# Two layers of grouped-query decode attention and a gated MLP: each 1 MB load of K and V issued as two transfers, of the even and of the odd partitions

## The chip, the cores and the metric

The kernel runs on one core of one Trainium2 chip. The metric is the device time of one execution in microseconds (us), the median of three runs. The profile is one further execution, recorded by the hardware profiler. Its times count from the first instruction of the program.

## What is computed

Four sequences each decode one token. A layer is attention over a cache of 4,096 positions (32 query heads, 8 heads of K and V, 128 wide) and a gated MLP, each behind a layer norm and with a residual. The two layers use the same weights and the same caches.

```python
def _A_ref(x, k_cache, v_cache, wq, wo):     # x (4, 1, 512); caches (4, 8, 4096, 128), bfloat16
    q = (x @ wq).reshape(B, Sq, Hq, Dh).transpose(0, 2, 1, 3)
    k = jnp.repeat(k_cache, rep, axis=1)
    v = jnp.repeat(v_cache, rep, axis=1)
    scores = jnp.einsum("bhqd,bhkd->bhqk", q, k) * (Dh ** -0.5)
    p = _softmax(scores, axis=-1)
    o = jnp.einsum("bhqk,bhkd->bhqd", p, v)
    return o.transpose(0, 2, 1, 3).reshape(B, Sq, Hq * Dh) @ wo

def _B_ref(x, w_gate, w_up, w_down):          # F = 1792
    h = _sigmoid(x @ w_gate) * (x @ w_up)
    return h @ w_down

x = x + _A_ref(_layernorm(x), k_cache, v_cache, wq, wo)
x = x + _B_ref(_layernorm(x), w_gate, w_up, w_down)
x = x + _A_ref(_layernorm(x), k_cache, v_cache, wq, wo)
x = x + _B_ref(_layernorm(x), w_gate, w_up, w_down)
```

K of one sequence and one head is 4,096 x 128 bfloat16 values, 1 MB, and so is V. There are 32 such pairs, and both layers read all of them.

## The kernel before, in words

A unit of work is one layer, one sequence and one head of K and V; the kernel has 64 units and takes them in pairs (32 pairs, written out in `ORDER`). The instructions of all engines are recorded by a small scheduler (`_Sched`), which turns reads and writes of named buffers into semaphore waits. The order of the steps within and between pairs is a string written by hand (`PROGRAM`), in which each letter is one step of one pair; the order of the loads is another string (`LOADS`: k, v, and o, g, u, d for weights).

One load fills one slot. A slot is 128 partitions of 4,096 values, that is 8 KB in each partition; position 32p + j of the cache lies in partition p, and so each partition's 8 KB is contiguous in HBM. There are 12 slots, and 4 more in the buffer of `wq` once layer two's queries are made (`yield_wq`, L978). Some K and V of layer one stay in their slots for layer two (`KEPT`); all others are read from HBM twice. That leaves 97 loads of 1 MB, each one transfer, and the very last V, which is read in two transfers of 512 KB, each of half the columns of all 128 partitions.

`pump` (L343) is called after every step. It takes loads from the list as long as a slot is free in the plan, and records each as one `dma_start` on SP's queue (L369) with the semaphore of its slot. All weight loads (L349 and, for `wq`, L382) are on the same queue. SP does nothing else. A load into a used slot waits on SP (its waits are recorded at L106) for the last reader of that slot: PE's score matmuls for K, PE's value matmuls for V. The queue is in order, and so a load that waits holds up all loads behind it.

The steps of one unit that touch a load:

- `k_turn` (L984, VectorE, L993) transposes the K slot in place in blocks of 32 x 32, in one to four parts. Its first part waits for the load of the slot.
- `scores` (L995, TensorE, L1009) multiplies the queries with K into PSUM; then the K slot is free.
- The maximum (L1026), its spreading (L1035), the bias (L1049, L1056), the exponential (ScalarE, L1063), the transpose of the probabilities (TensorE L1081, copies by ScalarE L1133) and the sums follow.
- `pv` (L1164, TensorE, L1179) multiplies the probabilities with V. Its first matmul waits for the V load; after its last one the V slot is free.

Between them lie the output projection (L1236, L1329), the MLP of layer one and the queries of layer two (L814, L839, L885, L934), which are done one sequence at a time beside the attention. After the last unit, the MLP of layer two ends the kernel.

The semaphore of a slot is raised by 16 by each transfer, one for each of the 16 DMA engines; `dma` (L82) records that, and `assign_values` (L85) counts what each waiter has to wait for.

Of the kernel before, what the change touches and what calls it, by code (L numbers as in the profile page):

```python
# [111 lines left out]


NSLOT = 12

# [28 lines left out]
def bass_interleave_layers__gqa_block_cached__glu_gated_glu__decode_kernel(  # L146
# [17 lines left out]
    P = 128  # L164
# [19 lines left out]
    S = _Sched()  # L184
# [4 lines left out]
    def sbt(shape, dtype, name):  # L189
        cnt[0] += 1  # L190
        return es.enter_context(nc.sbuf_tensor(f"{name}_{cnt[0]}", list(shape), dtype))
# [3 lines left out]

    slot = [sbt([P, NJ * DH], dt.bfloat16, f"slot{i}") for i in range(NSLOT)]
    wq_sb = sbt([P, KD, HQ * DH], dt.bfloat16, "wq")
# [20 lines left out]
    def small(*shape, dtype=dt.float32):  # L218
# [63 lines left out]
        list(ENGINES)  # L282
        + [f"d{i}" for i in range(NSLOT + KD)]
        + [f"wq{i}" for i in range(KD)]
# [51 lines left out]

    free = list(range(NSLOT))
    where = {}

    def take():  # L340
        return free.pop(0)

    def pump():  # L343
        while loads:
            kind, n = loads[-1]
            if kind in wparts:
                loads.pop()
                dst, src = wparts[kind](n)
                S.dma("sp", (lambda dst, src: lambda e: e.dma_start(dst, src))(dst, src), f"wo{n}" if kind == "wo" else kind, writes=[f"{kind}{n}"])  # L349
                continue  # L350
            if not free:
                return
            loads.pop()
            s = take()
            _, b, u = seq[n]
            if kind == "k":
                where["kn", n] = s
                src = A_k_cache[b, u].rearrange("(p j) d -> p (j d)", p=P)
            else:
                where["v", b, u] = s  # L360
                src = A_v_cache[b, u].rearrange("(p j) d -> p (j d)", p=P)
            parts = [(slot[s][:, :], src, f"d{s}", f"s{s}")]
            if kind == "v" and n == NU - 1:
                h = NJ * DH // 2
                parts = [(slot[s][:, 0:h], src[:, 0:h], "vh", "vh"), (slot[s][:, h:], src[:, h:], f"d{s}", f"s{s}")]
            for dst, frm, sem, key in parts:
                deps = S.readers.get(f"s{s}", []) + [S.last_write.get(f"s{s}")] if key == "vh" else ()
                S.dma(
                    "sp", (lambda dst, frm: lambda e: e.dma_start(dst, frm))(dst, frm), sem, writes=[key], deps=deps  # L369
                )  # L370

    def dve(fn, reads=(), writes=()):
        return S.inst("dve", fn, reads=reads, writes=writes)
# [5 lines left out]
    for n in range(KD // 2):  # L379
# [4 lines left out]
            writes=[f"wq{2 * n}", f"wq{2 * n + 1}"],  # L384
        )
    pump()

    S.inst("pool", lambda e: e.memset(qz_sb[:, :, :, :, :], 0.0), writes=QZ + ["pf"])
# [6 lines left out]
        writes=["pe0"],  # L395
    )
    dve(lambda e: e.transpose(pidx[:, :], iota_f[:, 0:32]), writes=["pe0"])
    for a in range(4):
# [6 lines left out]
            writes=[f"ident{a}"],  # L405
# [5 lines left out]
    for k in range(KD):  # L411
# [13 lines left out]
        writes=[f"x{b}" for b in range(Bn)],  # L425
# [552 lines left out]
    def yield_wq():  # L978
        for k in range(KD):
            S.last_write[f"s{NSLOT + k}"] = S.last_write[f"wq{k}"]  # L980
            S.readers[f"s{NSLOT + k}"] = list(S.readers[f"wq{k}"])
            free.append(NSLOT + k)

# [454 lines left out]
    head_masks()  # L1438
    k_turn(0)
    pump()  # L1440
    k_turn(1)
    pump()
    q_mm(Bn, 0, HQ)
    q_spread(0, Bn)
# [100 lines left out]
    for c in PROGRAM:  # L1545
# [29 lines left out]
        writes=["sel_row"],  # L1575
# [4 lines left out]
        writes=["rowk"],  # L1580
# [3 lines left out]
    for part in range(2):  # L1584
# [21 lines left out]
        writes=["o_row"],  # L1606
# [56 lines left out]
```

## Time and profile before

| | |
|---|---|
| three runs | 306.2, 306.71, 309.35 us; median 306.71 us |
| the profiled execution | 307.37 us, its span from the first to the last instruction 305.6 us |
| mean granted TensorE clock | 0.699 |
| busy: PE, DVE, ACT, POOL | 222.4, 193.8, 118.1, 40.3 us |
| read from HBM | 116.66 MB, 382 GB/s over the span |
| issues of 1 MB: V into slots, K into slots | 48, 44 |
| issues of 1 MB into the freed `wq` buffer: V, K | 3, 2 |
| issues of 512 KB of V | 2 |

How to read the profile. PE is TensorE's matmuls, DVE is VectorE, ACT is ScalarE, POOL is GpSimd, SP is the engine that issues the loads; a q behind a name (SPq) means the engine's sequencer, which waits and issues. L369 is line 369 of the kernel. The page cuts the span into 40 equal slices of 7.64 us; a digit is the busy share of a slice in tenths. A queue's line has packets, MB and the time that the packets took, as a share of the span of 16 engines. The chain of waits follows the work that ended last back to its start and gives each step's share of the span. A row of a table of stretches has the stretch, its length, then for PE, weight loads, DVE, ACT and POOL the busy us with the number of instructions, then the granted clock, the DMA engines' busy share and GB/s. A share of the DMA engines over 1 comes from packets whose recorded times overlap a little. A row of waits has the engine that waited and its line, what ended the wait, the us in total, how often, and the longest. The row of a line has the number of instructions and the shortest, median and longest duration in ns.

### The profile page before, as it was taken

To read this page: it belongs to the slowest core of one execution; us is meant where nothing else is said; L and a number is where in the kernel's file an instruction comes from. 1 tells how busy PE (TensorE), PEld (TensorE's weight loads), DVE (VectorE), ACT (ScalarE), POOL (GpSimd) and SP (SyncE) were. 2 spreads that over 40 slices of the span, in tenths; PEclk is the share of its full clock that TensorE was granted. 3 is DMA by queue.
4 is the path that set the end of the run, shared out by engine and by line. 5 is a ranking of instruction groups with operands and counts; after the bars stand their busy time and mean duration, and the time that the engine had idled before them with its cause. 6 is when DMAs were issued, how large, how long until landed. Compare 5 with 4: busy or idle time off the path is not lost.

```text
span 305.6 us, 11315 instructions
## 1 busy us (share of the span) xinstructions
PE 222.4 (73%) x4872; PEld 150.2 (49%) x4872; DVE 193.8 (63%) x414; ACT 118.1 (39%) x413; POOL 40.3 (13%) x205
## 2 busy tenths in 40 slices
PE   1223565147769699999899689885789799887886
PEld 1221243124636366647456556543556574564575
DVE  6344966254513587598946486757696777678443
ACT  1001152223503257731546625334466423557600
POOL 0002111001100212111113010112021010321000
PEclk9999999999995555557756556595555576657555
DMA  7999999999999999999999999999999999999930
GB/s 292 417 426 406 409 408 381 388 419 410 415 406 409 365 388 375 425 420 417 417 417 415 416 324 416 419 402 415 420 421 418 389 368 371 365 421 423 415 132 3
DMA packets 20361, 117.38 MB, mean 384 GB/s; under 512 B 1876, under 2 KB 5976, under 8 KB 7640
## 3 DMA queue, kind: packets, MB, share of 16 engines
q1 hardware_dynamic: 20288, 116.66, 95.0%
q8 instruction: 38, 0.62, 0.8%
q14 instruction: 11, 0.09, 0.1%
q10 hardware_dynamic: 24, 0.01, 0.0%
HBM read 116.66 MB, written 0.00 MB: 382 GB/s over the span
## 4 chain that ended last, share of the span: by engine, by line
DMA 50%; PE 29%; DVE 10%; issue 4%; SPq 3%; ACT 2%; POOL 1%; DVEq 0%; POOLq 0%; ACTq 0%
DMA slot<-in_A_v_cache_dram 18%; DMA slot<-in_A_k_cache_dram 15%; DMA wq<-in_A_v_cache_dram 11%; PE S_ps L1009 8%; DVE slot L993 8%; PE O_ps L1179 7%; DMA wd<-in_B_w_down_dram 6%; PE M_ps L885 3%; SPq L369 2%; PE M_ps L839 2%; PE M_ps L934 2%; DVE small L1026 1%; PE M_ps L814 1%; ACT pT L1133 1%; PE PT L1081 1%
## 5 line engine op out<-in xcount | busy, mean ns | idle before, releaser
L993 DVE STREAM_TRANSPOSE slot<-slot 128x1024 f32<-128x1024 f32 (+2 forms) x70 | 105.0, 1507 | 18.6 <-DMA slot<-in_A_k_cache_dram 15.3
L1133 ACT ACTIVATE pT<-PT 32x128 bf16<-32x128 f32 x236 | 63.1, 268 | 57.8 <-PE PT L1081 27.8
L1009 PE MATMUL S_ps<-slot,qz 128*16 128x256 bf16 x992 | 62.1, 398 | 18.3 <-DVE slot L993 8.1
L1179 PE MATMUL O_ps<-pT,slot 128*128 128x4 bf16 x1792 | 57.0, 166 | 21.2 <-DMA slot<-in_A_v_cache_dram 13.5
L1179 PEld LDWEIGHTS O_ps<-pT,slot 128*128 128x128 bf16 x1792 | 52.9, 103 | 34.9 <-DMA slot<-in_A_v_cache_dram 17.7
L1063 ACT ACTIVATE wide<-S_ps,small 128x256 bf16<-128x256 f32 x64 | 30.3, 473 | 44.6 <-DVE small L1056 18.9
L1009 PEld LDWEIGHTS S_ps<-slot,qz 128*16 128x16 bf16 x992 | 27.8, 113 | 39.1 <-DVE slot L993 10.7
L709 POOL COPY qz<-qs 32x32 bf16<-32x32 bf16 x128 | 26.0, 203 | 110.6 <-ACT qs L694 52.8
L1026 DVE TENSOR_REDUCE small<-S_ps 128x2 bf16<-128x512 f32 x32 | 21.7, 678 | 17.3 <-PE S_ps L1009 15.4
L1081 PE MATMUL PT<-ident_bf,wide 128*128 128x64 bf16 (+1 forms) x288 | 18.7, 227 | 3.4 <-ACT wide L1063 3.3
L1081 PEld LDWEIGHTS PT<-ident_bf,wide 128*128 128x128 bf16 x288 | 15.2, 122 | 10.0 <-ACT wide L1063 8.1
L1210 DVE TENSOR_TENSOR oT<-O_ps,small 128x8 bf16<-128x8 f32 (+1 forms) x32 | 5.3, 166 | 22.3 <-PE O_ps L1179 21.5
L1092 POOL CAST small<-small 128x2 bf16<-128x2 f32 x32 | 5.9, 184 | 99.0 <-ACT wide L1063 82.1
L1049 DVE SCALAR_TENSOR_TENSOR O_ps<-O_ps,small,wide 128x128 f32<-128x128 f32 x32 | 11.2, 349 | 8.7 <-PE O_ps L1035 6.8
L885 PE MATMUL M_ps<-wq,small 128*1 128x512 bf16 x128 | 14.6, 598 | 0.0
L1236 PE MATMUL AC<-wo,oT 128*1 128x512 bf16 x96 | 11.4, 576 | 2.1 <-DMA wo<-in_A_wo_dram 1.9
L1063 ACT ACTIVATION_READ_ACCUMULATOR wide<-S_ps,small 128x1 f32 x64 | 12.3, 193 | 0.0
L694 ACT ACTIVATE qs<-M_ps 128x128 bf16<-128x128 f32 x8 | 1.9, 280 | 25.0 <-PE M_ps L683 24.9
L1035 PE MATMUL O_ps<-ident_bf,small 128*128 128x64 bf16 x64 | 8.6, 225 | 4.1 <-DVE small L1026 1.8
L1056 DVE TENSOR_REDUCE small<-O_ps 128x2 f32<-128x128 f32 x32 | 9.3, 292 | 3.2 <-ACT wide L1063 0.5
L900 ACT ACTIVATE t_row<-M_ps,small 128x512 bf16<-128x512 f32 x4 | 2.7, 687 | 21.4 <-PE M_ps L885 18.7
L1147 PEld LDWEIGHTS O_ps<-small 128*128 128x128 bf16 x124 | 6.1, 107 | 7.7 <-POOL qz L709 1.7
(142 smaller groups left out, 209.4 us busy)
## 6 DMA issues: line engine op xcount, KB each, us to landing
slot<-in_A_v_cache_dram SPq DMA_DIRECT2D x48, 1024.0 KB, 9.8
slot<-in_A_k_cache_dram SPq DMA_DIRECT2D x44, 1024.0 KB, 11.4
wq<-in_A_wq_dram SPq DMA_DIRECT2D x2, 2048.0 KB, 10.0
wo<-in_A_wo_dram SPq DMA_DIRECT2D x8, 512.0 KB, 17.6
wq<-in_A_v_cache_dram SPq DMA_DIRECT2D x3, 1024.0 KB, 10.2
wq<-in_A_k_cache_dram SPq DMA_DIRECT2D x2, 1024.0 KB, 13.0
wu<-in_B_w_up_dram SPq DMA_DIRECT2D x2, 896.0 KB, 10.6
wg<-in_B_w_gate_dram SPq DMA_DIRECT2D x2, 896.0 KB, 10.6
```

The costliest lines, as they stand in the source:

```text
L709: (lambda a, ps: lambda e: e.tensor_copy(qz_sb[ps, :, :, a, :], qs_sb[b][ps, :, u * REP:(u + 2) * REP].rearrange("p t (u r) -> p u t r", r ...
L885: (lambda k, st: lambda e: e.matmul(M_ps[h][32 * st:32 * st + 1, :], lhsT=xc_bf[:, k, 0:1], rhs=wv[:, k, h, :, st, :], start=(k == 0), sto ...
L993: dve(lambda e: e.transpose(kf, kf), writes=[f"s{st}"])
L1009: (lambda t, b2, e_, c, x1, r0: lambda e: e.matmul(S_ps[p][r0:r0 + 4 * REP, half], lhsT=qz_sb[:, part, t, :, :].rearrange("p a r -> p (a r)"),
L1026: dve(lambda e: e.tensor_reduce(rm_bf, S_ps[p].rearrange("p (u n) -> p u n", u=2), AX.X, ALU.max), reads=[f"S{p}"], writes=["rmb"])
L1049: lambda e: e.scalar_tensor_tensor(out=shifted, in0=maxima, scalar=rowk_f, in1=mask_f.rearrange("p n w -> p (n w)").unsqueeze(1).broadcast ...
L1056: dve(lambda e: e.tensor_reduce(nm_sb, shifted, AX.X, ALU.min), reads=[f"O{n}"], writes=["nm"])
L1063: (lambda u, half: lambda e: e.activation(pe_sb[:, half], S_ps[p][:, half], ACTF.Exp, bias=nm_sb[:, u:u + 1], scale=exp_scale, accum_out=s ...
L1081: (lambda w, a0, a1, c0: lambda e: e.matmul(PT[:, c0:c0 + 16 * (a1 - a0)], lhsT=wide_sb[:, NV + 64 * w:NV + 64 * w + P], rhs=valid_bf[:, : ...
L1133: (lambda dst, frm: lambda e: e.activation(dst, frm, ACTF.Copy))(dst, frm),
L1179: (lambda n, x, c, j: lambda e: e.matmul(bank[:, ul * REP:(ul + 1) * REP], lhsT=vv[:, x * JG + c * 4 + j, :], rhs=pT[:, x % 2, ul, j, 2 * ...
L1236: (lambda r, h, i: lambda e: e.matmul(AC[32 * r:32 * r + 1, :], lhsT=oT_sb[:, h, own_column:own_column + 1], rhs=wo_sb[:, h, :], start=(j ...
```

## The change

Every 1 MB load of K and V becomes two `dma_start`s of 64 partitions each, first the even ones (0, 2, 4, ...), then the odd ones. Both are on SP's queue, one right behind the other, and both raise the semaphore of the slot by 16. The first carries the waits for the slot; whoever reads the slot waits for the count of the second. The last V keeps its two transfers of 512 KB. The weights' loads, the order of loads, slots and all other engines' instructions are the same.

```diff
+PIECES = 2
...
             for dst, frm, sem, key in parts:
                 deps = S.readers.get(f"s{s}", []) + [S.last_write.get(f"s{s}")] if key == "vh" else ()
-                S.dma(
-                    "sp", (lambda dst, frm: lambda e: e.dma_start(dst, frm))(dst, frm), sem, writes=[key], deps=deps
-                )
+                n = 1 if kind == "v" and len(parts) > 1 else PIECES
+                for h in range(n):
+                    rows = slice(h, P, n)
+                    issue = (lambda dst, frm: lambda e: e.dma_start(dst, frm))(dst[rows, :], frm[rows, :])
+                    if h == 0:
+                        S.dma("sp", issue, sem, writes=[key], deps=deps)
+                    else:
+                        S.last_write[key] = S.dma("sp", issue, sem)
```

## The prediction

> **What bounds the kernel now.** I read the page's busy line of the DMA engines first, then the queue totals, the chain, the stretches of time, and last what the issuing queue SP waits for.
>
> ```profile
> DMA  7999999999999999999999999999999999999930
> GB/s 292 417 426 406 409 408 381 388 419 410 415 406 409 365 388 375 425 420 417 417 417 415 416 324 416 419 402 415 420 421 418 389 368 371 365 421 423 415 132 3
> DMA packets 20361, 117.38 MB, mean 384 GB/s; under 512 B 1876, under 2 KB 5976, under 8 KB 7640
> ...
> q1 hardware_dynamic: 20288, 116.66, 95.0%
> ```
>
> The 16 DMA engines are busy in every slice but the last two, and SP's queue alone fills 95.0% of their span. Engines that never idle cannot be helped by more requests; only fewer or cheaper packets help. The chain says the same: half of it is transfers.
>
> ```profile
> DMA 50%; PE 29%; DVE 10%; issue 4%; SPq 3%; ACT 2%; POOL 1%; DVEq 0%; POOLq 0%; ACTq 0%
> DMA slot<-in_A_v_cache_dram 18%; DMA slot<-in_A_k_cache_dram 15%; DMA wq<-in_A_v_cache_dram 11%; PE S_ps L1009 8%; DVE slot L993 8%; PE O_ps L1179 7%; DMA wd<-in_B_w_down_dram 6%; PE M_ps L885 3%; SPq L369 2%; PE M_ps L839 2%; PE M_ps L934 2%; DVE small L1026 1%; PE M_ps L814 1%; ACT pT L1133 1%; PE PT L1081 1%
> ```
>
> The stretches show where the stream is full and where it runs short (last two columns: DMA share and GB/s).
>
> ```profile
> 92.00:120.00 28.00, 25.02 (x503) 15.20 (x502) 17.41 (x36) 12.26 (x43) 5.43 (x27) 0.50 0.99 381
> 120.00:172.00 52.00, 45.88 (x990) 30.63 (x991) 36.19 (x81) 25.98 (x90) 8.80 (x44) 0.60 1.01 418
> 172.00:186.00 14.00, 11.64 (x277) 8.82 (x274) 11.68 (x26) 6.10 (x21) 1.43 (x7) 0.61 0.96 362
> 186.00:240.00 54.00, 42.94 (x971) 28.82 (x972) 38.08 (x69) 25.47 (x91) 8.95 (x45) 0.57 1.01 417
> 240.00:266.00 26.00, 23.66 (x444) 14.64 (x445) 20.10 (x46) 10.04 (x34) 3.66 (x18) 0.63 0.96 365
> 266.00:292.00 26.00, 21.98 (x557) 16.05 (x549) 17.66 (x36) 16.10 (x59) 4.32 (x22) 0.57 1.01 418
> ```
>
> Full means 417 to 418 GB/s. Three stretches run short (381, 362, 365 GB/s): there the queue is nearly empty because SP waits for a slot that PE has not released. Against 417 they lose 28 x (1 - 381/417) = 2.4, 14 x (1 - 362/417) = 1.8 and 26 x (1 - 365/417) = 3.2 us, 7.5 us in all (rounded terms differ by 0.1). That is all that a change to the transfers could win there.
>
> ```profile
> SPq L106 <- PE O_ps L1179: 93.1, 36, 11.0
> SPq L106 <- PE S_ps L1009: 47.1, 16, 5.6
> ```
>
> SP spends 93.1 + 47.1 us of the span waiting for PE: it has time to spare for more issues.
>
> **The change, part by part.** 97 loads of 1 MB (48 + 44 into slots, 3 + 2 into the freed weight buffer) become 194 pieces of 64 partitions. The last V load, already two pieces of 512 KB, and all weight loads stay. The instruction order of SP's queue keeps each pair together, so nothing is moved past another transfer.
>
> *Packets.* In the trace's packet records an 8,192 B packet takes 309 ns (median of 12,433) and the 4 B packet that counts the semaphore 9 ns (median of 1,861). A load is 128 rows, 8 per engine: 8 x 309 + 9 = 2,481 ns. Its two pieces are 2 x (4 x 309 + 9) = 2,490 ns. So +9 ns a load on each engine, 97 x 9 = 0.87 us if every load lies in a full stretch. 24 loads are issued in the three short stretches, where the engines have gaps; without them it is 73 x 9 = 0.66 us. I take 0.9, since the loads around the stretches are full.
>
> *Is there a gap between two pieces?* The trace has one row near it: the last V load's two pieces of 512 KB. Their first engines' semaphore counts come at 289.51, 290.77 and 292.04 us (the load ahead, piece one, piece two): 1.26 and 1.27 us apart, against 8 packets of 4,096 B at 159 ns + 9 = 1.28 us. So consecutive transfers follow each other without a gap: zero. The upper bound is the start of an empty queue, issue at 0.72 us to first weight packet at 1.74 us, 1.0 us, 97 times = 99 us; the lower bound is 0. I take 0, since the pieces are queued like the row that shows none.
>
> [...]
>
> *SP's issues.* The issue of a load takes 0.33 us (median), and the next begins 0.05 us later.
>
> ```profile
> L369 SPq DMA_DIRECT2D slot<-in_A_v_cache_dram x48: 327/328/5861, 1.6 to 266.8; - x48
> L369 SPq DMA_DIRECT2D slot<-in_A_k_cache_dram x44: 327/328/10571, 2.2 to 261.5; - x44
> ...
> DMA to landing us min/median/max: 5.4/10.6/27.7
> ```
>
> 97 x 0.38 = 37 us more on SP, inside the 140 us that it waits. Two issues, 0.76 us, still hand over 1 MB faster than the engines move it (2.48 us), and a load lands a median 10.6 us after its issue, behind others. Where the queue is short, the second piece reaches the engines 0.38 us after the first, which has 4 x 309 = 1.24 us of data: the engines don't run out. Cost 0; bounds 0 and 24 x 0.38 = 9.1 us, if every load of the short stretches landed late by an issue. [...]
>
> *Waits.* DVE's transpose (L993) and PE's value product (L1179) now wait for the second piece's count, 32 a load instead of 16. Both pieces are needed, so the wait ends when the last of the 1 MB has landed, as before. Behind L993 stand DVE's reductions and PE's scores; they are late only by what the landing is late.
>
> *Instruction fetch.* The page's 38 fetches of 16 KB bring 0.62 MB for 11,315 instructions, 55 B each; 97 more are 5.3 KB, a third of a fetch, at about 1.0 us on one engine. Bounds 0 and 1.0 us; I take 0, as one engine's delay fades in the next short stretch.
>
> *Sum.* 0.9 + 0 + 0 + 0 = +0.9 us. The profiled execution took 307.37 us (span 305.6, 1.8 around it), so it would become 308.3; the median of the runs, 306.71, is 0.7 lower than that execution: 307.6 us.
>
> **The rivals.**
>
> *An exposed second issue (slower).* In the three short stretches each load reaches PE or DVE late, the slot is released late, and the next load is issued late. Price up to 9.1 us: 306.7 + 0.9 + 9.1 = 316.7. For it: there SP's issues follow PE's releases, and PE is busy 89% in the first and 91% in the last. Against it: 0.38 is less than 1.24. It decides if the second piece starts later than the first one's data ends, above 1.24 us. Chance 0.12.
>
> *Pieces that don't stream at full rate (slower).* No transfer of 64 partitions stands in this trace, so how its rows are dealt to engines is not shown. If two engines met at one place of the memory throughout, each row would take twice as long: 97 x 2.48 = 241 us more, 548 us; a gap of 1.0 us gives 406 us; a rate lost by a tenth 24 us, 332 us. Against it: the 512 KB pieces and every other shape here stream back to back. It decides if 8,192 B packets rise above 309 ns by more than 4 ns (1.3%, 3 us). Chance 0.07.
>
> [...]
>
> *A quicker restart (faster).* After an idle moment, first packets take up to 1.6 us instead of 0.309 (around 179.6 us). If half-size transfers get started sooner and win half of the 7.5 us, it is 306.7 + 0.9 - 3.7 = 303.9. Against it: the consumer still waits for both pieces, and the wait for the memory is not shortened. Chance 0.08.
>
> That the split is not carried out is excluded: SP's list of the changed kernel has the pairs, 64 x 4096 each.
>
> **How the numbers follow.** The forecast case has 0.70, at 306 to 309.5; 0.03 is left for scatter beyond that. About 1% (3.1 us) is what a measurement of this kernel can tell from no change: its three runs lie between 306.2 and 309.35. Slower by over 1%, above 309.8: the second rival whole, 0.07, most of the first, 0.10, and 0.02 of scatter, 0.19. Faster, below 303.6: most of the third, 0.06 (with 0.01 of scatter). Within 1%: the rest, 0.75. The range, 304 to 313, takes in the forecast, most of the quicker restart and the lower half of the exposed issue, and leaves out about 0.15.
>
> **What would show it.** Right: 8,192 B packets still 309 ns; about 1,550 more 4 B packets (97 x 16); full stretches at 415 to 418 GB/s; SP's waits for PE shorter by about 37 us; landings of paired pieces 1.24 us apart. Wrong: rates below 410 GB/s in the full stretches (second rival); short stretches that grow while the full ones stay (first rival); short stretches that vanish (third).

## The result, and the profile after

The changed kernel takes 308.38 us (median of 20 runs, 306.24 to 310.57); the kernel before, run beside it, takes 306.69 us (20 runs). The ratio is 1.0069, with a 95% interval from 1.0046 to 1.0092: 0.0069 x 306.69 = 2.1 us more, between 1.4 and 2.8 us. The ratio leaves out executions that lie more than 1.5% above the fastest of their kernel; the medians lie 1.7 us apart, and the means of all 20 runs of each kernel (308.55 and 307.09 us) 1.5 us. That is less than the 1% that the prediction calls no change, but the interval is clear of 1. The predicted 307.6 us is 0.8 us below the measured median.

The profiled execution of the changed kernel took 310.57 us, the slowest of its 20, with a span of 308.7 us; that of before took 307.37 us. Their difference of 3.2 us is therefore larger than that of the medians, and where a stretch differs by a microsecond between the two, part of it is scatter.

The page of the changed kernel, the lines of the DMA engines and of SP's queue:

```profile
DMA  7999999999999999999999999999999999999920
GB/s 294 418 425 410 408 405 379 390 419 401 406 412 378 360 382 364 418 423 382 419 408 361 425 340 418 420 356 415 418 419 420 418 392 383 379 428 420 411 82 3
DMA packets 21914, 117.40 MB, mean 380 GB/s; under 512 B 3428, under 2 KB 7528, under 8 KB 9192
...
q1 hardware_dynamic: 21840, 116.67, 94.5%
```

Packets under 512 B grew from 1,876 to 3,428. That is 1,552 = 97 x 16, one more 4 B packet for each load on each engine, and nothing else changed in size. In the packet records the 8,192 B packets still take 309 ns (median of 12,434) and the 4 B ones 9 ns (median of 3,413). At before's median for each size, a mean engine of before has 278.6 us of SP's packets, and one of after 279.5 us.

The same six stretches of the changed kernel (length, then PE, weight loads, DVE, ACT and POOL, the clock, the DMA share and GB/s):

```profile
92.00:120.00 28.00, 25.21 (x503) 15.45 (x503) 17.42 (x37) 12.08 (x43) 5.43 (x27) 0.50 0.98 372
120.00:172.00 52.00, 42.99 (x934) 28.48 (x934) 35.96 (x81) 25.20 (x89) 8.79 (x44) 0.63 1.00 401
172.00:186.00 14.00, 11.97 (x274) 8.86 (x275) 10.08 (x24) 7.04 (x24) 1.43 (x7) 0.53 0.98 374
186.00:240.00 54.00, 43.26 (x989) 28.99 (x986) 39.32 (x69) 24.36 (x88) 8.57 (x43) 0.59 1.00 410
240.00:266.00 26.00, 22.41 (x444) 14.66 (x445) 18.57 (x44) 9.30 (x31) 3.23 (x16) 0.63 0.98 389
266.00:292.00 26.00, 21.04 (x495) 14.47 (x487) 17.79 (x32) 16.35 (x60) 4.76 (x24) 0.57 1.01 421
```

The rate is lower in three stretches (372, 401, 410 GB/s) and higher in the other three: the moments with a nearly empty queue lie elsewhere. Two cuts through the middle of the full stretches show such moments, at a DMA share of 1.00 and 0.98 where before had 1.01 and 1.00 (418 and 406 GB/s):

```profile
132.00:146.00 14.00, 11.95 (x253) 7.62 (x251) 11.89 (x25) 3.96 (x13) 1.09 (x6) 0.62 1.00 400
200.00:212.00 12.00, 9.49 (x217) 5.37 (x210) 8.01 (x13) 5.12 (x18) 2.00 (x10) 0.78 0.98 372
```

SP's view, first the issues (shortest, median, longest in ns), then its waits for PE:

```profile
L372 SPq DMA_DIRECT2D slot<-in_A_v_cache_dram x96: 471/596/5508, 1.7 to 273.8; - x96
L372 SPq DMA_DIRECT2D slot<-in_A_k_cache_dram x88: 471/597/5032, 3.0 to 268.3; - x88
...
DMA to landing us min/median/max: 3.9/9.2/21.5
```

```profile
SPq L106 <- PE O_ps L1185: 59.3, 25, 9.7
SPq L106 <- PE S_ps L1015: 37.0, 15, 4.6
```

An issue of 64 partitions takes 0.47 us behind a wait and 0.60 us behind another issue, where one of 128 took 0.33 us behind a wait and 0.43 us and up right behind another (16 of K and V, median 0.55 us). A load thus holds SP for 0.47 + 0.05 + 0.60 = 1.12 us, not the 0.33 + 0.05 + 0.33 = 0.71 us that the prediction's figures give. SP's waits for PE at L106 shrank from 140.2 to 96.3 us. SP still has time over.

### The profile page after: what moved, and what is told of

It reads as the page before. It is cut to its first block, busy times and chain, and to the rows that moved or that the text cites. A ratio compares the mean times of both kernels' runs of the same rounds, so it can differ in the third digit from the quotient of the medians.

```text
span 308.7 us, 11412 instructions
## 1 busy us (share of the span) xinstructions
PE 220.8 (72%) x4872; PEld 149.6 (48%) x4872; DVE 193.6 (63%) x414; ACT 118.1 (38%) x413; POOL 40.3 (13%) x205
## 4 chain that ended last, share of the span: by engine, by line
DMA 45%; PE 24%; DVE 14%; SPq 8%; issue 4%; ACT 2%; POOL 1%; DVEq 0%; POOLq 0%; ACTq 0%
DMA slot<-in_A_k_cache_dram 19%; DMA slot<-in_A_v_cache_dram 18%; DVE slot L999 10%; PE O_ps L1185 7%; PE S_ps L1015 7%; SPq L372 6%; DMA wd<-in_B_w_down_dram 5%; DMA wq<-in_A_v_cache_dram 3%; PE M_ps L891 2%; SPq L350 2%; ACT pT L1139 2%; DVE small L1032 1%; PE O_ps L1335 1%; POOL qz L715 1%; PE AC L1268 1%
## 5 line engine op out<-in xcount | busy, mean ns | idle before, releaser
L999 DVE STREAM_TRANSPOSE slot<-slot 128x1024 f32<-128x1024 f32 (+2 forms) x70 | 105.0, 1507 | 19.7 <-DMA slot<-in_A_k_cache_dram 16.4
L1015 PE MATMUL S_ps<-slot,qz 128*16 128x256 bf16 x992 | 60.2, 391 | 17.4 <-DVE slot L999 9.2
L1015 PEld LDWEIGHTS S_ps<-slot,qz 128*16 128x16 bf16 x992 | 26.7, 111 | 37.8 <-DVE slot L999 12.4
L1087 PEld LDWEIGHTS PT<-ident_bf,wide 128*128 128x128 bf16 x288 | 15.3, 122 | 10.1 <-ACT wide L1069 8.2
## 6 DMA issues: line engine op xcount, KB each, us to landing
wo<-in_A_wo_dram SPq DMA_DIRECT2D x8, 512.0 KB, 16.4
wq<-in_A_v_cache_dram SPq DMA_DIRECT2D x8, 512.0 KB, 14.1
```

The costliest lines, as they stand in the source:

```text
L999: dve(lambda e: e.transpose(kf, kf), writes=[f"s{st}"])
L1015: (lambda t, b2, e_, c, x1, r0: lambda e: e.matmul(S_ps[p][r0:r0 + 4 * REP, half], lhsT=qz_sb[:, part, t, :, :].rearrange("p a r -> p (a r)"),
L1087: (lambda w, a0, a1, c0: lambda e: e.matmul(PT[:, c0:c0 + 16 * (a1 - a0)], lhsT=wide_sb[:, NV + 64 * w:NV + 64 * w + P], rhs=valid_bf[:, : ...
```

## The theories

*Packets alone* (the prediction): the 4 B packets cost 97 x 9 ns, 0.9 us, and everything else is hidden. *SP's time*: the longer issues make loads late where the queue is short, and that is the rest of the 2.1 us. *Half rate*: pieces of 64 partitions move at half the rate of whole loads, the prediction's second rival.

## The experiments

Each ratio is to the kernel before, run on the same chip beside it, with its 95% interval.

### SP's time alone, half a microsecond a load

```diff
                 S.dma("sp", ..., sem, writes=[key], deps=deps)
+                if len(parts) == 1:
+                    S.group("sp", [lambda e: [e.wait_ge(sems["xin"], 16) for _ in range(17)] and None])
```

> The kernel before with whole loads, and after each of the 97 loads SP executes 17 waits that are already satisfied, about 47 ns each in the trace of after (17 ns and a gap of 30), so 0.8 us more on SP a load, about what the split adds there (0.47 + 0.60 + 0.05 us in place of 0.33). No packet is added. If SP's longer issues are what made the change cost more than its packets: 1.001 to 1.006 of the time before. If only the packets cost: 1.000, within 0.002.

Measured: 308.32 us, ratio 1.0038 (1.0003 to 1.0073). Two waits went into one instruction, and so the loss was 0.5 us a load and not 0.8: an estimate from nine instructions at 0.06 us, the time that each of thirteen takes in SP's records of the kernel with 26 waits ahead of all 97 loads, below (0.77 us from 136.30 to 137.07 us). The value is in the range of SP's time, but the interval almost reaches 1. These waits stand behind a load and ahead of SP's wait for the next slot, so they use SP's time without making a load late that SP has to wait for: SP's waits for PE at L106 are 83.9 us here, 140.2 before.

### Four pieces

`PIECES = 4`, so `rows = slice(h, P, 4)`: 32 partitions a piece.

> Four pieces of 32 partitions a load (every fourth partition). If only the 4-byte packets cost, 27 ns a load more than before, 97 times: 2.6 us, ratio 1.0085. If SP's issues count: four issues of about 0.6 us are 2.5 us a load, as long as its 2.48 us of transfer, so SP can no longer refill the queue after a wait for a slot and becomes the bound: at least 10 us more than before, ratio over 1.03, with the engines no longer full between 120 and 172 us.

Measured: four runs of 318.9 to 326.3 us, median 324.55, with 307.07 before; they scatter too far for an interval. At least 11.8 us more, against 2.6 us of packets. The page of this kernel has 1,876 + 97 x 3 x 16 = 6,532 packets under 512 B, 8,192 B packets still at 309 ns, and SP at its limit:

```profile
L372 SPq DMA_DIRECT2D slot<-in_A_v_cache_dram x192: 468/594/5012, 1.7 to 295.8; - x192
L372 SPq DMA_DIRECT2D slot<-in_A_k_cache_dram x176: 468/594/2971, 4.2 to 284.7; - x176
```

```profile
120.00:172.00 52.00, 44.41 (x928) 28.66 (x920) 36.69 (x80) 23.93 (x84) 8.87 (x44) 0.57 0.99 384
```

```profile
SPq L1617 <- DVE slot L1608: 14.4, 1, 14.4
SPq L106 <- PE O_ps L1185: 9.7, 7, 5.8
```

Its waits for PE are down from 140 us to about ten, issues back to back fill its queue, and the stretch that was full at 418 GB/s has 384. So SP has almost no time left at four issues a load; how much of the loss that explains is taken up below, with the kernels of more waits.

### Two pieces by columns

```diff
-                    rows = slice(h, P, n)
-                    issue = (lambda dst, frm: lambda e: e.dma_start(dst, frm))(dst[rows, :], frm[rows, :])
+                    w = NJ * DH // 2
+                    cut = slice(h * w, (h + 1) * w) if n > 1 else slice(0, w)
+                    issue = (lambda dst, frm: lambda e: e.dma_start(dst, frm))(dst[:, cut], frm[:, cut])
```

> Two pieces a load by columns: all 128 partitions, 4,096 B of each. The packets then take 2 x (8 x 159 + 9) = 2,562 ns a load in place of 2,481, so 97 x 81 ns = 7.9 us more by the packets alone: ratio 1.022 to 1.026. If two issues a load cost something beside it, over 1.026. The issues of 128 contiguous partitions should be as short as before (0.33 us, 0.43 us back to back) if the partition step makes the pieces' issues long.

Measured: 315.77 us, ratio 1.0254 (1.0189 to 1.0319), 7.8 us (5.8 to 9.8; the medians lie 8.7 us apart), where the packets alone give 7.9. The way of counting packets holds within those 2 us; the closer agreement is luck. The issues took 0.33 us, and 0.43 us back to back: 128 partitions were issued faster than 64 (0.47 and 0.60 us), with rows of 4,096 B as with rows of 8,192 B.

### Two pieces of adjacent partitions

`rows = slice(h * P // n, (h + 1) * P // n)`: partitions 0 to 63, then 64 to 127.

> Two pieces a load of partitions 0 to 63 and 64 to 127. If the place of the rows doesn't matter: as the change, 307 to 310 us. [...] The issues show whether a contiguous set of 64 partitions is issued in 0.33 us or in 0.47 and 0.60 us as the even and odd ones.

Measured: 497.75 us, one run, with 307.07 before: 191 us more. The page:

```profile
GB/s 340 232 232 239 230 223 218 223 227 225 375 239 217 223 228 231 227 229 228 231 243 241 233 251 250 253 248 243 246 263 274 280 261 229 221 221 227 231 225 13
DMA packets 21914, 117.40 MB, mean 237 GB/s; under 512 B 3428, under 2 KB 7528, under 8 KB 9192
...
q1 hardware_dynamic: 21840, 116.67, 97.6%
```

The packets are the same in number and size as in the changed kernel; 8,192 B packets now take 574 ns (median) and not 309, and the rate falls to 217 to 280 GB/s while K and V are read. 97 x 8 x (574 - 309) ns = 206 us, about what was lost. So which 64 partitions a piece has sets its rate here: 574 ns a packet for adjacent ones, near the rival of half rate, and 309 ns for even and odd ones. What slows the adjacent ones is not shown.

### The split where the queue is short, and where it is full

```diff
+SHORT = {*range(23, 35), *range(54, 59), *range(80, 87)}
-                n = 1 if kind == "v" and len(parts) > 1 else PIECES
+                n = PIECES if len(parts) == 1 and (nth[0] in SHORT) else 1
+                nth[0] += 1
```

and `not in SHORT` for the second kernel.

> The change for 24 loads only: those that the profile of before issues in the three short stretches (92 to 120, 172 to 186, 240 to 258 us). If the second piece and the longer issues make loads late where the queue is nearly empty: +1.0 to +2.5 us, ratio 1.003 to 1.008. If only the packets cost: 24 x 9 ns = 0.2 us, ratio 1.000 to 1.002.

> The change for the other 73 loads, which are issued while earlier transfers still fill the queue. Packets: 73 x 9 ns = 0.7 us, ratio 1.002. If late issues cost only where the queue is nearly empty, no more than that: 1.000 to 1.004. If SP's lost time counts in the full stretches too (the queue has less in it when SP next has to wait): 1.004 to 1.008.

Measured: short stretches alone 307.8 us, ratio 1.0034 (0.9998 to 1.0069); all others alone 307.74 us, ratio 1.0007 (0.9977 to 1.0037). Neither is clear of 1. Added they give 0.41%, with an interval of about 0.47% to each side (the two half-widths combined as a root of squares), which holds both 0.28% of packets and the measured 0.69%. The order of the two is that of SP's time theory, but their intervals overlap, and by the medians (306.67 us before) they cost the same, 1.1 us each.

### Whole loads with 0.8 us of waits on SP ahead of each, in the short stretches, in the others, in all

```diff
+                late = 26 if len(parts) == 1 and nth[0] in SHORT else 0
-                    "sp", (lambda dst, frm: lambda e: e.dma_start(dst, frm))(dst, frm), sem, writes=[key], deps=deps
+                    "sp",
+                    (lambda dst, frm, late: lambda e: (
+                        [e.wait_ge(sems["xin"], 16) for _ in range(late)], e.dma_start(dst, frm)
+                    )[1])(dst, frm, late),
+                    sem, writes=[key], deps=deps,
```

with `not in SHORT` for the second and no condition for the third.

> Whole loads; the same 24 loads are each issued about 0.8 us late, by 26 satisfied waits on SP after the wait for the slot (two are packed into an instruction, 0.06 us each). No packet is added. If a late issue is exposed in the short stretches: between 2 us (every tenth of it) and 19 us (all of it), ratio 1.007 to 1.06. If the queue hides it there: within 0.3% of before.

> Whole loads; the other 73 loads are each issued about 0.8 us late, 58 us of SP's time. If a late issue costs only where the queue is nearly empty: within 0.3% of before. If lost time on SP counts wherever SP waits for slots: 1.005 or more.

> Whole loads, each of the 97 issued about 0.8 us late by 26 satisfied waits on SP: the time that the change adds on SP, before the load itself, and no packet. If SP's time is what the change costs beyond its packets (0.69% measured, 0.28% packets): ratio 1.002 to 1.006. If the packets and something else in the transfers cost all of it: 1.000 to 1.002.

Measured: 1.0026 (0.9992 to 1.0059), 1.0018 (0.9987 to 1.0049) and, for all, 1.0016 (0.9983 to 1.0049). For all 97 loads the upper end is 0.49%.

These runs did not do what was expected of them. In the program that ran, SP's wait for the slot stands behind the satisfied waits, just ahead of the load. One load of the kernel with all 97 shows it in SP's records: from 136.30 us on come thirteen satisfied waits of 17 to 28 ns, at 137.07 us one that takes 2,231 ns because it also holds PE's semaphore, and at 139.34 us, 0.04 us after its end, the issue. The profile counts that wait among the added ones: the longest on their line takes 10 us, and SP's waits for PE stand there too, 100.8 us of them in place of 140.2.

```profile
L372 SPq EVENT_SEMAPHORE  x1326: 17/28/10049, 2.4 to 269.8; - x190
```

```profile
SPq L372 <- PE O_ps L1184: 61.3, 29, 10.1
SPq L372 <- PE S_ps L1014: 39.5, 16, 5.4
```

So a load that SP has to wait for was not made late by the added waits; they took their time out of SP's wait. Of the 24 loads of the short stretches SP waited for the slot of all 24 before, and still for 17 here; all 17 were issued within 0.11 us of the wait's end. The other 7 found their slot free, and how late they were the records don't tell. The time in which such waits held SP ahead of the 24 (those over 0.11 us in its records) went from 67.5 to 47.6 us, by about the 19 us that the waits add. With waits ahead of all 97 loads it went from 169 to 108 us. What the three kernels show is that SP can lose 0.8 us a load ahead of its waits for less than 0.6% of the time. What it costs when a load that SP waits for goes out late, once its slot is free, they don't show. Only the kernels with pieces have that, and there 24 split loads in the short stretches cost at most 0.69%.

### More waits

The last kernel with 46 and with 69 waits.

> The same with 46 waits, about 1.4 us a load: SP then needs 1.8 us a load against 2.48 us of transfer. If the cost grows in proportion to SP's lost time: 0.7 to 1.0%. If it grows faster once SP has little time over: 1 to 3%.

> The same with 69 waits, about 2.1 us a load: SP then needs 2.5 us a load, as with four pieces, and as long as the transfer. If the 17 us of the four pieces come from SP's time, all but their 2.6 us of packets: 12 to 17 us more than before, ratio 1.04 to 1.055. If they come from the smaller pieces in the transfer engines: under 1.02.

Measured: 46 waits cost 1.0131 (1.0097 to 1.0164), 69 waits 1.0207 (1.0145 to 1.0269), 6.4 us. Here too the wait for the slot comes last. The cost is below 0.5% at 0.8 us a load and 1.0 to 1.6% at 1.4 us. Waits for slots hold SP for 67 and 21 us, ahead of 36 and 17 of the 97 loads (71 before); the others find their slot free when SP reaches them.

The kernel with 2.1 us needs as much SP time a load as that with four pieces, but loses 6.4 us (4.5 to 8.3), where the four pieces lose at least 11.8 - 2.6 = 9.2 us beside their packets. So some 3 us (1 to 5) of the four pieces' loss, or more, is not SP's lost time as these waits make it. Two differences could account for that, and neither was tried by itself. The pieces stand behind the wait for the slot, and the added waits ahead of it. And each piece hands over 2 x 309 + 9 = 627 ns of work, less than the 640 ns from one issue to the next (a median 594 ns and the 0.05 us behind it), so engines could run dry between pieces, an estimate from these figures.

### The change with 0.8 us of waits ahead of each load

The changed kernel with 26 waits ahead of each first piece. The wait for the slot again stands behind them.

> The change, and each load's first piece issued about 0.8 us late by 26 satisfied waits. If the longer issues of the pieces use up the same spare time of SP as the waits do, SP loses 0.8 + 0.8 = 1.6 us a load: between the 1.3% of 1.4 us and the 2.1% of 2.1 us, about 1.5%, and 0.3% of packets, 1.6 to 2.0% over before. If the change's cost beyond its packets lies in the transfers and not on SP: its 0.7% and the 0.2% that 0.8 us cost with whole loads, 0.7 to 1.1%.

Measured: 307.4 us, ratio 1.0017 (0.9977 to 1.0057). Both forecasts miss: SP's time theory wanted 1.6 to 2.0%, the other 0.7 to 1.1%, and the upper end is 0.57%. Its page shows that the waits and pieces are there, and SP's longest waits:

```profile
SPq L378 <- PE O_ps L1192: 27.5, 12, 7.9
SPq L1624 <- DVE slot L1615: 22.5, 1, 22.5
SPq L378 <- PE S_ps L1022: 11.5, 11, 2.9
```

SP waits for PE about 40 us and not 140, having lost 1.6 us a load, and the kernel is no slower than the split alone. So SP's total time is not, by itself, what costs: waits for slots hold it for 45 us here and for 67 us in the kernel with 46 waits, yet that one loses 1.0 to 1.6% and this one at most 0.6%. Why they differ stays open.

This kernel holds the whole change, and its 1.0017 lies below the 1.0028 of the packets alone. The change itself was measured in one set of 20 runs and not again beside the later kernels, so part of its 1.0069 may be scatter.

## Why the prediction was right, point by point

- *Packets, +0.9 us.* Right as a count: 1,552 more 4 B packets at 9 ns, and rows unchanged at 309 ns. That such a count gives the time is borne out by the column pieces, 7.8 us (5.8 to 9.8) where it gives 7.9; 0.9 us alone is too little for these runs to show.
- *No gap between pieces.* Right: near the start, with 12 transfers outstanding, the first engines' counts of successive pieces come at 13.65, 14.89 and 16.13 us, 1.24 us apart, which is 4 x 309 + 9 ns. These are among the closest: over the 97 pairs the median is 1.50 us, and so the sign of paired pieces 1.24 us apart did not hold in general. But what a pair takes more, the step to the next load takes less: in the full stretch from 266 to 292 us the first counts of successive loads lie a median 2.48 us apart in both kernels. The bound of 1.0 us a piece is out.
- *SP's issues, 0.38 us a piece, hidden.* The size was wrong, the verdict right. A piece takes 0.47 or 0.60 us, and the sum of SP's issues rose from 96.6 to 161.5 us, 65 us and not 37. (These sums include 14 issues of over 1 us before, 56.1 us, and 27 after, 56.4 us. The 14 began with 6 to 10 transfers outstanding, and so did 19 shorter ones; what held them is not shown.) It fitted into SP's waits for PE, which fell by 44 us (37 forecast). SP's time spent ahead of those waits cost under 0.6% at 0.8 us a load in three kernels, and 0.03 to 0.73% at 0.5 us in a fourth. What made the step right is the wide margin of 140 us, and not the estimate. Not shown to be hidden is what comes behind a wait for a slot, which after's trace has ahead of 49 loads: the first issue takes 0.14 us longer, and the second piece is issued 0.51 us after the first (median).
- *Waits.* Right: DVE's transposes waited 16.4 us for K in after's profiled execution and 15.3 in before's: a wait for the second piece's count ends about as the wait for the whole load did.
- *Instruction fetch.* Right: 38 fetches of 16 KB before and after.
- *The sum.* 0.9 us against 2.1 (1.4 to 2.8). The forecast case's range of 306 to 309.5 us holds the median, but the sum lies below the interval. The step that is short is the sum of zeros, by 1.2 us (0.5 to 1.9), or by 0.6 to 0.8 us if the means or medians of all runs are compared. Where this rest lies can't be read from the traces. In the two profiled executions, from the first weight packet at 1.74 us to the end of the last load the engines spend 14.1 us beyond their packets before and 16.2 us after. But in the other kernels with packets within 1 us of these, this figure is 12.7 (split in the full stretches), 12.8 (split in the short), 13.2, 13.3 and 15.6 (0.8 us of waits ahead of the 73, all and the 24 loads), 13.6 (split and waits) and 14.9 us (17 waits behind each load): executions differ by more than what is sought. Since neither half of the split, nor the split with waits, is clear of 1, the cause of the rest stays open. Loads handed over later behind SP's waits, and scatter, are both possible.
- *The rivals.* The exposed second issue was priced at up to 9.1 us and given 0.12: the change as a whole costs at most 2.8 us, and the split of the 24 loads alone at most 0.69% (2.1 us), packets included. So the full price is out; a small part of it is not. The kernels with added waits don't bear on it, since a load that SP waits for is not late in them. Packets at near half rate came with adjacent halves (574 ns) and not with even and odd rows (309 ns). The quicker restart did not come: no kernel here was measurably faster than before.
- *A sign that misled.* The prediction said that full stretches below 410 GB/s would show pieces at a lower rate. After has 401 GB/s in one of them (120 to 172 us) with packets at a median 309 ns. What it has more of are 8,192 B packets over 600 ns, 35 where before has 15, like those after the idle moment near 179.6 us: that points to empty moments in the window. The median duration of a packet was 309 ns in that window before and after; the window's GB/s, 418 and 401, took in the idle time too.

## What to carry to other kernels

When transfers bound a kernel, count its packets by size and duration: that gave the cost of loads cut by columns as 7.9 us, and 7.8 (5.8 to 9.8) were measured. Splitting a load cost little here (ratio 1.0069) where the packets kept their 309 ns, as those of even and odd partitions did, and the issuing queue handed over bytes faster than they moved (1.12 us of issues a load against 2.48 us of packets); two issues a load left that queue spare time, four left almost none, and two halves of adjacent partitions, at 574 ns a packet, cost 191 us. Where several terms are nil by argument, give their sum an error of its own: here it was some 0.6 to 1.2 us that no single experiment could place. And look in the trace for a delay that an experiment puts in: here it stood ahead of a wait that took it up.

## What the runs showed of the hardware that was not expected

Transfers of fewer partitions took longer to issue: 128 partitions 0.33 us behind a wait and from 0.43 us right behind another issue (with rows of 8,192 or 4,096 B), 64 partitions 0.47 and 0.60 us, whether even, odd or adjacent, and 32 partitions a median 0.59 us. And satisfied waits put between a load and its wait for the slot in the source stood ahead of that wait in the program that ran, so that 0.8 us of them a load cost less than 0.6%.
